# The half tile of features in the first products of the gated layer and of the experts, multiplied with 128 rows

## The chip, the cores and the metric

The kernel runs on one core of a Trainium2 chip. The core has five engines that run side by side, each with its own queue: TensorE (PE in the rows; its weight loads are listed apart as PEld), VectorE (DVE), ScalarE (ACT), GpSimd (POOL) and SyncE (SP). The metric is the device time of one launch in microseconds (us); lower is better. Times shown are medians of several runs; the profile is of one execution.

## The reference

Three layers follow each other on 4 batches of 768 tokens with 320 features.

```python
# 1. per head (8 heads of 40): a recurrence over the tokens
y[:, :, t] = einsum('bhd,bhde->bhe', rt, state)
Sa = einsum('bhde,bhe->bhd', state, at)
state = state * wt - outer(Sa, bt) + outer(vt, kt)
# 2. gated layer
h = maximum(x @ w_in, 0); u, v = h[..., :512], h[..., 512:]
v_n = (v - mean(v)) / sqrt(var(v) + 1e-6)
v_s = einsum('ts,bsd->btd', w_spatial, v_n) + b_spatial
x = (u * v_s) @ w_out
# 3. experts: the logits (with a local gate) choose one of 8 for each token
h = maximum(x[b, s] @ w1[e], 0)          # 320 -> 1024
out[b, s] = p[e] * (h @ w2[e])           # 1024 -> 320
```

The change concerns the two products whose contraction runs over the 320 features: `x @ w_in` and `x @ w1[e]`.

## The kernel before

**How a product is made exact enough.** The kernel multiplies in a shortened float32 format (float32r in the code). To keep float32's accuracy each operand is split into a high part, which the format holds, and a low part, the rest: x = xh + xl, W = WH + WL. A product is then the sum of three matmuls into one accumulator, WH xh + WL xh + WH xl; the term WL xl is left out.

**The 320 features** are two full tiles of 128 rows and half a tile of 64. The half tile is packed: the weights' tile 2 holds WH in its rows 0 to 63 and WL of the same features in rows 64 to 127, and the tokens' tile 2 holds the same 64 features twice. One matmul of 128 rows over (tile 2 of W, xh[2]) therefore gives WH xh + WL xh at once. What is missing is WH xl, and it is a second matmul over the rows 0 to 63 alone. So every group of first products has eight matmuls: three for each of the full tiles, one of 128 rows and, as the last, one of 64 rows.

**Where these groups stand.**
- Gated layer, `Gmlp.terms` (lines 796 to 804). `vprod` makes the v half, 128 tokens by 512 columns, six times per batch. `upart` makes the u half, 128 features of h by 384 tokens, eight times per batch. The matmuls' line in the profile is 795, that of the helper `mm`.
- Experts, `Moe.experts` (lines 1164 to 1294). A slot is 256 tokens of one expert (full) or 128 tokens (half); 17 slots always run, 12 full and 5 half, in the order F F, five times F F H, then further half slots that run only if they are needed. A full slot has eight groups of eight matmuls, one for each 128 rows of h, with the weights stationary and the 256 tokens moving (line 1245); then two products back to 320 columns, 24 matmuls each (`e_py`). A half slot has two groups of eight with the tokens stationary and 512 columns of weights moving (line 1264), four transposes for each, and one product back. The matmuls' line is 1200, that of the helper `products`.

**Tiles.** In the profile the gated layer's tokens go by reused buffers: xh are A32x, A32y, X32x and xl are X32y and two parts of XT1x, the second of which is xl[2]. The experts' tokens are xh and xl, the weights eWH and eWL, made from raw. The accumulators are pv, pu (gated layer, two buffers each), e_ph (four buffers) and e_py (two).

**What the other engines do beside it.** In the gated layer `splits` (line 735) makes xh on ScalarE and xl on VectorE (line 737); for the half tile xl is computed in rows 0 to 63 only, and rows 64 to 127 keep the unsplit features. v is normalized on VectorE (`vnorm`) and split again (`vsplit`: g_vh on ScalarE, g_vl on VectorE or GpSimd, line 837); the gated product `gated(i)` reads all six row blocks of g_vh and g_vl in order. In the experts `turn` transposes the gathered tokens of the next slot and splits them, with all 128 rows of xl[2]. A group of e_ph leaves through ScalarE (hh, line 1246) and VectorE (hl, line 1247). The weights of the slot after next are fetched by an indirect transfer (line 1173) and split in five pieces, each by a cast on ScalarE (line 1161) and a subtraction on VectorE (lines 1162 and 1163), put between the groups of the slot ahead.

**Order.** The attention's order is made by a list scheduler; the gated layer and the experts run in the order in which the code is written (`manual_schedule`), each engine taking its own instructions in turn.

Of the kernel before, what the change touches and what calls it, by code (L numbers as in the profile page):

```python
# [8 lines left out]
F32 = mybir.dt.float32  # L9
# [5 lines left out]
ALU = mybir.AluOpType  # L15
# [8 lines left out]
WW,AA,KB=0,264,520   # columns of the e-major record  # L24
EW=1032

def layout(r,k,v,w,a,b):
    """host: layout only"""
    f=np.float32
    def ch(x):  # (B,H,S,D)->(B,NC,pair,h,C,D)  # L30
        return x.reshape(B,NP,2,NC_,C,D).transpose(0,3,1,2,4,5)
    rc,kc,vc,wc,ac,bc=map(ch,(r,k,v,w,a,b))
    dm=lambda x: x.transpose(0,1,3,5,2,4)  # B,NC,h,D,pair,C
    e=np.zeros((B,NC_,RE,EW),f)
    # w: a zero, and per pair 64 values and a zero
    for h in range(2):
        rows=slice(64*h,64*h+40)
        we,ae,be,ke=(dm(x)[:,:,h] for x in (wc,ac,bc,kc))
        wz=np.zeros((B,NC_,40,NP,65),f); wz[...,:64]=we
        e[:,:,rows,WW+1:WW+261]=wz.reshape(B,NC_,40,260)  # L40
        e[:,:,rows,AA:AA+256]=ae.reshape(B,NC_,40,256)
        s0,s1=(be,ke) if h==0 else (ke,be)
        kb=np.stack([s0,s1],axis=4)  # B,NC,40,pair,slot,C
        e[:,:,rows,KB:KB+512]=kb.reshape(B,NC_,40,512)
    pw=np.ones((NP,65),f); pw[:,64]=0
    e[:,:,40:64,WW+1:WW+261]=pw.reshape(-1)
    # d-major: columns per pair V^T | R^T
# [6 lines left out]
    # t-major v of head 2p+1, with 16 rows of zeros after it, and of head 2p, with 16 before it  # L54
# [6 lines left out]
def attention(ctx,tc,ed,dd,vd,yT,order,K=KEYS,wp=None,prep=None,ident=None,guard=None):  # L61
    """ed,dd,vd as layout() gives; yT dram [320, B*S]"""
# [15 lines left out]
    ut=cp.tile([128,104],F32,name="ut")         # -1, in the first 64 columns only where s < t  # L78
# [37 lines left out]
    def heat(bank):  # L116
        # keeps the array's clock up while there is nothing to do
        if bank not in hcur: hcur[bank]=ps.tile([128,256],F32,name=bank)
        nc.tensor.matmul(out=hcur[bank],lhsT=hz[:,0:128],rhs=hz,start=True,stop=True)
    def tied(bank,n):  # L120
        # the same, but not before operation n has run
# [9 lines left out]
    nc.scalar.copy(hs,hz[:,0:2])       # has the engine's table loaded  # L131
# [7 lines left out]
    # ---- what does not depend on the state, chunk q of all heads of a batch  # L139
# [30 lines left out]
    def stM(q):  # L170
        # Q^T only; of A' the inversion reads nothing but what lies over its diagonal
# [14 lines left out]
    def stA(q):  # L186
        # once A' has left for the inversion, A-hat takes its place under (over) Q^T
        for sl,r in enumerate(halves): nc.scalar.copy(LQ[q][r,sl],AB[q%NAB][r,:,sl,:])
    # ---- inversion of the triangular matrices of n8 chunks
    def t32(ss):  # L190
# [7 lines left out]
        def load():  # L198
            # unit = (f, h, g, p); the 32x32 blocks on the diagonal
# [4 lines left out]
        def loadn():  # L204
            # and the block above
# [17 lines left out]
        def xtr():  # L223
            nc.scalar.copy(A32[ss][0:HU],X32[ss][0:HU].rearrange("p s t -> p t s"))   # A32 has done its work
# [17 lines left out]
    # ---- the chain of the chunks  # L242
# [91 lines left out]
    # ---- order: every engine takes, when it is free, the most urgent of what is ready by the estimates below  # L334
# [12 lines left out]
    if guard is not None:  # L347
        # in the room that the second inversion will take
# [67 lines left out]
    # list scheduling  # L416
# [11 lines left out]
    cols=dict(stQ=1672,stT=677,vr=324,s=643,z=1332,c1=78,c2=165,w=1644,t=845,y=1700)   # columns that the clock's monitor counts  # L428
# [12 lines left out]
    bank={b:-1. for b in ("pvr","pw","pc","pq","pk")}     # free since  # L441
# [48 lines left out]
    if K.get("xh"):  # L490
        # more of them where the chip waits longer than the estimates say
# [22 lines left out]
# attention() divides by the products of up to 64 decays: these must stay far from under- and overflow.  # L514
# A sum of exp(32 w) and one of exp(-32 w) over GN values bound each of them to 0.51 .. 1.29; values between 0.75 and 1.05 always pass.
# [3 lines left out]
def guard(nc,cp,wd):  # L519
    """(name, engine, time, after, time of transfer, function): whether any decay is out of the range, as an integer in flag"""  # L520
# [26 lines left out]
def general(ctx,tc,raw,yT,ident):  # L547
    """attention() for any decays: step by step, the state of 10 rows of a head on a partition"""
# [41 lines left out]
XW=392     # row of the token table: x2 | its last 64 columns again | 8 probabilities  # L590
# rows of x^T: tile 0 = heads 0,2,4 and 8 rows of head 6, tile 1 = heads 1,3,5 and 8 rows of head 7, tile 2 = the rest of 6 and 7
FEAT=np.concatenate([np.arange(40*h,40*h+n)+o for h,n,o in ((0,40,0),(2,40,0),(4,40,0),(6,8,0),(1,40,0),(3,40,0),(5,40,0),(7,8,0),(6,32,8),(7,32,8))])

def glayout(w_in,w_sp,b_sp,w_out,w_gate,w_local):
    f=np.float32
    # float64 goes as its bits
    wi=np.ascontiguousarray(w_in).view(np.int64)[FEAT]
    win=np.stack([wi[0:128],wi[128:256],np.concatenate([wi[256:320],wi[256:320]])],axis=1)  # 128,3,1024
# [5 lines left out]
class Gmlp:  # L604
# [4 lines left out]
    def narrow(self,src,raw,m,e,l):  # L609
        """src: dram, [128, n] bits of float64; its value as a sum of two float32, in m and l: (engine, name, function) by function"""  # L610
# [15 lines left out]
    def early(self,tmp):  # L626
        """the preparation that fits beside the end of the attention: (name, engine, time, after, time of transfer, function)"""
# [4 lines left out]
        def slot(tag): # what frees the next slot of the tag, and the operation that took the one before it  # L632
# [5 lines left out]
        def wi(k,h):  # L638
            """512 columns of a row tile of w_in"""
# [32 lines left out]
        def ws(c,n):  # L672
            """384 columns of a row tile of w_spatial"""
# [18 lines left out]
        # x of the first batch, where the inversions were  # L692
# [20 lines left out]
    def lload(self):  # L713
        """the last of w_spatial, where u will be"""
# [6 lines left out]
    def loads(self,b,eng=None):  # L721
        """x^T of a batch from y: (function, number of transfers)"""
# [12 lines left out]
    def splits(self,k):  # L735
        nc=self.nc; n=128 if k<2 else 64
        def lo(): nc.vector.tensor_tensor(out=self.xl[k][0:n],in0=self.xl[k][0:n].bitcast(F32),in1=self.xh[k][0:n].bitcast(F32),op=ALU.subtract)
# [5 lines left out]
    def weights(self,c1,gp):  # L743
        """what is left of the preparation; c1: context of what only the products before w_out need, gp: pool of the rest"""
# [5 lines left out]
        # the bias, on every partition  # L750
# [3 lines left out]
    def wout(self,ident,room):  # L754
        """w_out, with its product with the gate's weights beside it: (function before a product, function with it) four times"""
# [40 lines left out]
    def terms(self,tok,ff,tok_first):  # L796
# [6 lines left out]
        r+=[(xh[2],WH[2]),(xl[2][0:64],WH[2][0:64])]  # L803
        return r if tok_first else [(w,x) for x,w in r]
    def vprod(self,j):
        """the rows of 128 tokens before their normalization"""
# [17 lines left out]
    def vnorm(self,j):  # L824
# [4 lines left out]
        # 1/sqrt(var+eps), with a Newton step  # L829
# [13 lines left out]
    def biased(self,i):  # L843
        """what the products of gated(i) are added to"""
# [3 lines left out]
    def gated(self,i,gg,between=None):  # L848
        """between: what the array does next"""
# [13 lines left out]
    def out_(self,px,j,c,mid=None):  # L863
        """mid: what the array does in between"""
# [4 lines left out]
    def logits(self,LG,h,ident,lt):  # L869
        """LG [128,6,10]: the logits, and the local gate's, of half of the tokens"""  # L870
# [10 lines left out]
    def outp(self,j,xr,LG=None,mid=None):  # L881
        """xr [128,6,XW]: rows of the token table"""
# [8 lines left out]
SL=256            # tokens of a full slot  # L891
VE=3072//SL       # slots an expert can have
NF=12             # full slots
NH,NHA=8,5        # slots of half the tokens: at most, and those that always run
# [4 lines left out]
def mlayout(w1,w2):  # L899
    """(8*128, WC): per expert and partition, three tiles of rows of w1 (the last 64 rows twice) and eight of w2"""  # L900
# [4 lines left out]
class Moe:  # L905
# [10 lines left out]
    def fill(self):  # L916
# [21 lines left out]
        self.tok=cp.tile([128,24],F32,name="tok")      # 1 + the token's number  # L938
# [3 lines left out]
    def fill2(self):  # L942
        nc=self.nc; cp=self.tp
        # of the slots: bounds of the number in the list; number among the half slots and which half of a group (0 for the full ones)
# [19 lines left out]
    def route(self,b,LG,xr):  # L964
        """the stages of the routing of a batch: [what the vector engine begins with, then in turn products and what follows them]"""
# [8 lines left out]
        def begin(h):  # L974
# [8 lines left out]
            # the first of the largest logits  # L983
# [4 lines left out]
            # hold: 1/(1+exp(-z)) < 0.5 fails; in float32 that is 1+exp(-z) <= 2, and exp(-z) = 1-z where it matters  # L988
# [4 lines left out]
            # (8+fr)*(1-hold)  # L993
# [9 lines left out]
        def rows(n):  # L1003
            # half of the tokens, as two rows
# [17 lines left out]
        def places():  # L1022
            # place among the expert's tokens
# [28 lines left out]
    def first(self):  # L1052
        """the tokens of the first slot"""
# [9 lines left out]
    def heat(self,n,pu=None):  # L1063
        """products that nobody reads keep the array's clock up while it waits"""
        if pu is None: pu=self.ps.tile([128,384],F32,name="pu")
        for _ in range(n): self.nc.tensor.matmul(out=pu,lhsT=self.idb,rhs=self.i256.bitcast(BF16)[:,0:384],start=True,stop=True)
    def slots(self):
        """Which tokens and which expert a slot has. A list holds every expert's groups of 256 tokens (where the last may lack up to 127),
        then the rests of up to 128. The full slots take the list from its beginning; the half slots go on: two for a group, one for a rest."""
# [7 lines left out]
        # the first slot is the first expert's even if it has no tokens  # L1077
# [7 lines left out]
        # what the number in the list lacks to the number of the place  # L1085
# [15 lines left out]
    def slots2(self):  # L1101
# [4 lines left out]
        # the expert  # L1106
# [6 lines left out]
        # rows of the expert's weights; none where the buffer has them already  # L1113
# [6 lines left out]
        # the place  # L1120
# [13 lines left out]
    def numbers(self,ps):  # L1134
# [4 lines left out]
        # where the tokens are read from and written to; 4095 where there is none  # L1139
# [10 lines left out]
    def prefetch(self):  # L1150
        """the weights of the first slot"""
# [12 lines left out]
    def experts(self,ctx,out):  # L1164
# [36 lines left out]
        def run(lo,hi):  # L1201
            todo=[]
            def prepare(s):
                """the pieces of a slot's weights, to be split beside the slot before"""
# [24 lines left out]
            for s in range(lo,hi):  # L1229
# [7 lines left out]
                if n==2:  # L1237
                    for j in range(8):
# [6 lines left out]
                        products(ph,t+[(WH[:,c],xh[:,2]),(WH[0:64,c],xl[0:64,2])])  # L1245
# [6 lines left out]
                else:  # L1252
                    # the tokens stay in the array, the weights pass
# [3 lines left out]
                    for q in range(2):  # L1257
# [6 lines left out]
                        products(ph,t+[(xh[:,2,tk],WH[:,c]),(xl[0:64,2,tk],WH[0:64,c])])  # L1264
# [217 lines left out]
```

## Time and profile before

| | us |
|---|---|
| median of 3 runs | 1062.14 |
| lowest and highest run | 1059.57, 1075.4 |
| span of the profiled execution | 1064.1 |
| TensorE busy in it | 996.2 |
| VectorE busy | 752.6 |
| ScalarE busy | 585.2 |
| GpSimd busy | 444.6 |

The span goes from the first to the last instruction of one profiled execution; the page gives no other time for it. The busy time of TensorE counts overlapping matmuls once, and a matmul's end is modelled, so a busy TensorE can still be one that advances slowly: the distance between the starts of successive matmuls says how fast it goes. "PEclk" is the granted clock of TensorE as a share of full speed. An arrow in brackets names what ended an engine's idle time.

### The profile page before, as it was taken

What the parts mean: (1) busy time and instruction counts of PE and PEld (TensorE: products, weight loads), DVE (VectorE), ACT (ScalarE), POOL (GpSimd) and SP (SyncE); (2) the same over time, 40 slices, a digit from 0 to 9 for tenths busy, and PEclk for the clock granted to TensorE, in tenths of its full rate; (3) what the DMA queues carried; (4) which work ended last, traced back from release to release, by engine and by line L of the source; (5) the groups of instructions that cost most, each with busy time, mean ns of one, the idle gap of its engine ahead of it and who ended that gap; (6) DMA issues with size and microseconds to landing.
All of it is one profiled execution on the core that took longest, in us unless ns stands there. A gap on an engine that the chain in (4) does not pass through costs nothing. (4 is left out here: it accounts for less than half of the span.)

```text
span 1064.1 us, 25293 instructions
## 1 busy us (share of the span) xinstructions
PE 996.2 (94%) x9524; PEld 843.2 (79%) x9524; DVE 752.6 (71%) x2076; ACT 585.2 (55%) x1309; POOL 444.6 (42%) x624
## 2 busy tenths in 40 slices
PE   7898988888988999999999999999999999999995
PEld 6677777677877778876888888888878889888884
DVE  8989869998795999665765535654556666766672
ACT  7556656666766777773444324333435556655561
POOL 7886755756494621550431060220453232233211
PEclk8778978997977999999999999999999999999998
DMA  8756684765857664535200302101275643632530
GB/s 206 188 128 173 132 178 104 165 153 144 158 129 154 150 134 93 137 83 147 70 1 1 91 1 45 47 1 46 109 257 206 242 158 126 248 128 97 230 126 15
DMA packets 179055, 133.05 MB, mean 125 GB/s; under 512 B 132989, under 2 KB 165631, under 8 KB 177264
## 3 DMA queue, kind: packets, MB, share of 16 engines
q1 hardware_dynamic: 173376, 84.13, 33.2%
q0 software_dynamic: 5552, 47.25, 12.0%
q8 instruction: 77, 1.26, 0.5%
q14 instruction: 50, 0.41, 0.1%
HBM read 113.54 MB, written 27.26 MB: 132 GB/s over the span
## 5 line engine op out<-in xcount | busy, mean ns | idle before, releaser
L219 DVE TENSOR_TENSOR pr<-A,X 128x30 f32<-128x30 f32 (+40 forms) x427 | 114.8, 307 | 4.1 <-POOL AB L161 3.3
L222 DVE TENSOR_TENSOR X<-X,pr 128x30 f32<-128x30 f32 (+40 forms) x427 | 112.3, 302 | 0.2
L1163 DVE TENSOR_TENSOR eWL<-raw,eWH 128x1024 fp32r<-128x1024 f32 (+1 forms) x64 | 86.4, 1358 | 33.7 <-ACT eWH L1161 33.4
L1161 ACT CAST eWH<-raw 128x1024 fp32r<-128x1024 f32 (+1 forms) x85 | 94.0, 1134 | 0.0
L1290 POOL DMA_INDIRECT out_dram<-yo,sid x29 | 29.6, 1020 | 147.5 <-ACT yo L1289 108.1
L1200 PE MATMUL e_ph<-xl,eWH 128*128 128x256 f32 (+1 forms) x288 | 90.5, 314 | 0.2 <-DVE xl L1191 0.2
L1200 PE MATMUL e_ph<-xh,eWH 128*128 128x256 f32 x288 | 89.9, 312 | 0.0
L173 POOL TENSOR_SCALAR_AFFINE_SELECT lq<-lq 64x256 f32<-64x256 f32 x96 | 67.2, 700 | 50.8 <-DMA pu<-lq 29.6
L157 POOL TENSOR_TENSOR kb<-etile,Ft 104x256 f32<-104x256 f32 x88 | 71.3, 830 | 41.1 <-DVE D L149 24.6
L1200 PE MATMUL e_py<-eWH,hh 128*128 128x320 f32 x232 | 73.0, 315 | 0.0
L322 PE MATMUL py<-X,kt 128*64 128x104 f32 x384 | 56.1, 286 | 17.9 <-DVE X L317 17.9
L1200 PE MATMUL e_py<-eWH,hl 128*128 128x320 f32 x232 | 72.3, 312 | 0.2 <-DVE hl L1273 0.2
L1200 PE MATMUL e_py<-eWL,hh 128*128 128x320 f32 x232 | 71.6, 309 | 0.0
L1246 ACT ACTIVATE hh<-e_ph 128x256 fp32r<-128x256 f32 x96 | 37.0, 385 | 62.6 <-PE e_ph L1200 61.3
L1247 DVE SCALAR_TENSOR_TENSOR hl<-e_ph,hh 128x256 fp32r<-128x256 f32 x96 | 39.6, 422 | 42.8 <-ACT hh L1246 42.8
L857 PE MATMUL pv<-sh,g_vh 128*128 128x384 f32 x192 | 67.1, 350 | 0.0
L161 POOL TENSOR_TENSOR AB<-etile,GP 64x256 f32<-64x256 f32 x82 | 62.9, 767 | 7.2 <-issue 2.2
L857 PE MATMUL pv<-sl,g_vh 128*128 128x384 f32 x192 | 64.8, 337 | 0.0
L857 PE MATMUL pv<-sh,g_vl 128*128 128x384 f32 x192 | 64.7, 337 | 0.0
L1200 PEld LDWEIGHTS e_ph<-xl,eWH 128*128 128x128 f32 (+1 forms) x288 | 53.9, 187 | 12.7 <-DVE xl L1191 0.4
L165 PE MATMUL pq<-AB,kb 104*128 104x128 f32 x384 | 63.7, 318 | 0.1
L1200 PEld LDWEIGHTS e_ph<-xh,eWH 128*128 128x128 f32 x288 | 54.0, 187 | 11.6 <-DVE eWH L1162 0.3
(350 smaller groups left out, 2984.5 us busy)
## 6 DMA issues: line engine op xcount, KB each, us to landing
etile<-in_ed_dram SPq DMA_DIRECT2D x48, 419.2 KB
DT<-in_dd_dram SPq DMA_DIRECT2D x96, 80.0 KB
pu<-lq SPq DMA_DIRECT2D x96, 80.0 KB
yT<-yt SPq DMA_DIRECT2D x48, 104.0 KB
X<-in_vd_dram SPq DMA_DIRECT2D x96, 50.0 KB
XT<-in_w_dram SPq DMA_DIRECT2D x10, 384.0 KB
xs<-xr SPq DMA_DIRECT2D x3, 1176.0 KB
praw<-in_win_dram SPq DMA_DIRECT2D x6, 512.0 KB
```

The lines of the kernel that those rows point to most:

```text
L157: eng.tensor_tensor(out=kb[:,:,sl,:],in0=kbr[:,:,sl,:],in1=FT[q][:,::-1,63::-1],op=ALU.mult)
L161: eng.tensor_tensor(out=AB[q%NAB][r,:,sl,:],in0=ar[r],in1=GP[q%NBIG][r,:,0:64],op=ALU.mult)
L165: nc.tensor.matmul(out=PQ[q][:,p,:],lhsT=kbt[q][:,p].rearrange("p s t -> p (s t)"),rhs=AB[q%NAB][0:RE,p].rearrange("p s t -> p (s t)"),sta ...
L173: nc.gpsimd.affine_select(out=LQ[q][r,h],in_=LQ[q][r,h],pattern=[[0,NP],[1,64]],**sel)
L219: nc.vector.tensor_tensor(out=pv,in0=a[0:U,0:t,t:t+1].to_broadcast([U,t,c1-c0]),in1=x[0:U,t:t+1,c0:c1].to_broadcast([U,t,c1-c0]),op=ALU.mult)
L222: nc.vector.tensor_tensor(out=x[0:U,0:t,c0:c1],in0=x[0:U,0:t,c0:c1],in1=pv,op=ALU.subtract)
L322: nc.tensor.matmul(out=py[0:64,p,:],lhsT=KT[q][:,p,0:64],rhs=x[:,p,0,:],start=False,**acc)
L857: for j,(l,r) in enumerate(t): nc.tensor.matmul(out=pv,lhsT=l,rhs=r,start=False,stop=j==len(t)-1,skip_group_check=True)
L1161: nc.scalar.copy(WH[:,c0:c1],raw[:,c0:c1])
L1163: else: V.tensor_tensor(out=WL[:,lc(c0):lc(c1)],in0=raw[:,c0:c1],in1=WH[:,c0:c1].bitcast(F32),op=ALU.subtract)
L1200: for i,(l,r) in enumerate(t): nc.tensor.matmul(out=out,lhsT=l,rhs=r,start=i==0,stop=i==len(t)-1)
L1247: V.scalar_tensor_tensor(out=hl[:,j],in0=ph,scalar=0.0,in1=hh[:,j].bitcast(F32),op0=ALU.max,op1=ALU.subtract)
```

## The change

The matmul of the half tile's low part takes 128 rows of both operands and not 64. In its rows 64 to 127 it adds WL xl for the half tile's features, the term that is left out elsewhere. In the gated layer the subtraction that makes xl[2] runs over 128 rows too, so that these rows hold low parts; in the experts they did already. The number and the order of the instructions on every engine stay the same; four subtractions of line 737 (and a fifth that runs only in the fallback for extreme decays) and 162 matmuls with their weight loads change their number of rows. The rest of the diff removes comments.

```diff
@@ Gmlp.splits, line 735
-        nc=self.nc; n=128 if k<2 else 64
-        def lo(): nc.vector.tensor_tensor(out=self.xl[k][0:n],in0=self.xl[k][0:n].bitcast(F32),in1=self.xh[k][0:n].bitcast(F32),op=ALU.subtract)
+        nc=self.nc
+        def lo(): nc.vector.tensor_tensor(out=self.xl[k],in0=self.xl[k].bitcast(F32),in1=self.xh[k].bitcast(F32),op=ALU.subtract)
@@ Gmlp.terms, line 803
-        r+=[(xh[2],WH[2]),(xl[2][0:64],WH[2][0:64])]
+        r+=[(xh[2],WH[2]),(xl[2],WH[2])]
@@ Moe.experts, full slot, line 1245
-                        products(ph,t+[(WH[:,c],xh[:,2]),(WH[0:64,c],xl[0:64,2])])
+                        products(ph,t+[(WH[:,c],xh[:,2]),(WH[:,c],xl[:,2])])
@@ Moe.experts, half slot, line 1264
-                        products(ph,t+[(xh[:,2,tk],WH[:,c]),(xl[0:64,2,tk],WH[0:64,c])])
+                        products(ph,t+[(xh[:,2,tk],WH[:,c]),(xl[:,2,tk],WH[:,c])])
```

## Rows read from the trace of the kernel before

**Rows 1.** The page of the profiled execution: its span.

```profile
span 1064.1 us, 25293 instructions
```

**Rows 2.** Busy time by stretch: us, then each engine (x instructions), granted clock, DMA, GB/s.

```profile
492.50:1051.50 559.00, 552.91 (x3223) 471.53 (x3224) 336.48 (x758) 265.21 (x504) 154.61 (x211) 1.00 0.32 111
510.60:522.50 11.90, 11.90 (x56) 9.08 (x56) 11.24 (x28) 7.10 (x17) 5.81 (x14) 1.00 0.02 4
```

**Rows 3.** TensorE's timeline, experts, full slot: start us, duration us, engine, line, output and operands.

```profile
802.43 0.31 PE L1200 MATMUL e_py<-eWH,hl 128*128 128x320 f32 x1
802.58 0.28 PE L1200 MATMUL e_ph<-xh,eWH 128*128 128x256 f32 x1
...
803.29 0.28 PE L1200 MATMUL e_ph<-xh,eWH 128*128 128x256 f32 x1
803.50 0.38 PE L1200 MATMUL e_ph<-xl,eWH 64*128 64x256 f32 x1
803.81 0.39 PE L1200 MATMUL e_ph<-xh,eWH 128*128 128x256 f32 x1
804.03 0.28 PE L1200 MATMUL e_ph<-xl,eWH 128*128 128x256 f32 x1
```

**Rows 4.** Groups by line and shape, the matmuls of 64 rows: busy us, mean ns.

```profile
L1200 PE MATMUL e_ph<-xl,eWH 64*128 64x256 f32 x96 | 36.6, 382 | 0.0
...
L795 PE MATMUL pu<-XT1x,wh 64*128 64x384 f32 x32 | 14.1, 441 | 0.0
...
L795 PE MATMUL pv<-wh,XT1x 64*128 64x512 f32 x24 | 11.9, 496 | 0.0
...
L1200 PE MATMUL e_ph<-eWH,xl 64*128 64x512 f32 x10 | 5.0, 496 | 0.0
```

**Rows 5.** TensorE's timeline, last u product of the first batch and the gated product behind it.

```profile
520.62 0.34 PE L795 MATMUL pu<-X32y,wh 128*128 128x384 f32 x1
...
521.31 0.34 PE L795 MATMUL pu<-X32x,wh 128*128 128x384 f32 x1
521.58 0.44 PE L795 MATMUL pu<-XT1x,wh 64*128 64x384 f32 x1
521.95 0.44 PE L857 MATMUL pv<-sh,g_vh 128*128 128x384 f32 x1
522.23 0.33 PE L857 MATMUL pv<-sl,g_vh 128*128 128x384 f32 x1
```

**Rows 6.** TensorE's timeline, experts, a half slot.

```profile
858.43 0.40 PE L1200 MATMUL e_ph<-eWH,xh 128*128 128x512 f32 x1
858.75 0.50 PE L1200 MATMUL e_ph<-eWH,xl 64*128 64x512 f32 x1
...
859.51 0.39 PE L1200 MATMUL e_ph<-eWH,xl 128*128 128x512 f32 x1
...
860.67 0.40 PE L1200 MATMUL e_ph<-eWH,xh 128*128 128x512 f32 x1
```

**Rows 7.** Line 737 by tile: durations min/median/max ns, first and last start, shapes.

```profile
L737 DVE TENSOR_TENSOR XT1x<-XT1x,A32y x4: 950/954/958, 490.5 to 673.2; 128x768 fp32r<-128x768 f32 x4
L737 DVE TENSOR_TENSOR XT1x<-XT1x,X32x x4: 940/941/944, 491.8 to 677.3; 64x768 fp32r<-64x768 f32 x4
```

**Rows 8.** GpSimd's timeline, first batch: the last low part for gated(0).

```profile
523.13 1.29 POOL L837 TENSOR_TENSOR g_vl<-g_v,g_vh 128x512 fp32r<-128x512 f32 x1 [2.24 <-ACT g_vh L836]
```

**Rows 9.** The page's costliest groups: busy us, mean ns, idle before and its releaser.

```profile
L1163 DVE TENSOR_TENSOR eWL<-raw,eWH 128x1024 fp32r<-128x1024 f32 (+1 forms) x64 | 86.4, 1358 | 33.7 <-ACT eWH L1161 33.4
...
L1247 DVE SCALAR_TENSOR_TENSOR hl<-e_ph,hh 128x256 fp32r<-128x256 f32 x96 | 39.6, 422 | 42.8 <-ACT hh L1246 42.8
```

**Rows 10.** Transfers into the tiles raw from 760 us on.

```profile
DMA to landing us min/median/max: 2.1/10.7/11.5
```

**Rows 11.** GpSimd's timeline: the issue of one slot's weights.

```profile
921.95 1.01 POOL L1173 DMA_INDIRECT raw<-in_wt_dram,wid  x1 [3.73 <-DVE eWL L1163]
```

**Rows 12.** ScalarE's timeline: the first read of these weights.

```profile
937.18 1.04 ACT L1161 CAST eWH<-raw 128x1024 fp32r<-128x1024 f32 x1
```


## The prediction, made before the result was known

> **What bounds the kernel now.** I read the busy time by stretch first. From 492.5 us, where the first product of the gated layer starts, to 1051.5 us, where the last product of the experts ends, TensorE is busy 552.91 of 559.00 us, at a granted clock of 1.00 (the 2.4 GHz level) throughout; VectorE is busy 336 us of it and ScalarE 265 us [rows 2]. The span is 1064.1 us [rows 1]. So in this stretch what TensorE does not have to do leaves the span, as long as the engines with 60% and 47% keep up.
>
> A busy TensorE need not be a productive one, so the second view is its timeline, read by starts and not by durations (matmuls overlap). Within a group of e_ph the starts of 256-column matmuls are (803.29 - 802.58)/6 = 0.118 us apart [rows 3]. Then comes the matmul that the change edits, xl against eWH with 64 rows: it starts 0.21 us after its predecessor, the next one 0.31 us after it, and the one behind that 0.22 us later [rows 3]. Three steps that would take 0.354 us at the normal pace take 0.74: **0.386 us are lost around one matmul of 64 rows**. A group's end is not the cause: from the last e_py to the first e_ph, another group, another tile, both with 128 rows, it is 0.15 us, no more than the 320 columns need [rows 3]. Nor is it a wait for xl: two of the six steps between 802.58 and 803.29 begin 128-row matmuls of xl.
>
> The same hole is there at other widths and with operands exchanged. 384 columns, in the u products: normal pace (521.31 - 520.62)/4 = 0.173; from 521.31 to 522.23 it is 0.92 against 0.519, a loss of 0.40 [rows 5]. 512 columns, in a half slot, where the tokens are stationary: normal (860.67 - 859.51)/5 = 0.232; from 858.43 to 859.51 it is 1.08 against 0.696, a loss of 0.384 [rows 6]. The loss does not grow with the columns: it is a fixed price for going from 128 rows to 64 and back. I take 0.39 us.
>
> **The change part by part.** No instruction is added, removed or moved. The second operand pair of one product per group gets 128 rows, and the split of xl[2] in the gated layer does 128 rows, so that the other 64 hold low parts and not unsplit features (in the experts they are split already).
>
> *The matmuls.* There are 96 + 32 + 24 + 10 = 162 of them [rows 4]. With 128 rows each has the form of its neighbours, which run without the hole. What they still cost is the neighbours' pace, already in the 0.354. So 162 x 0.39 = 63.2 us: 106 in the experts (41.3) and 56 in the gated layer (21.8). Bounds: 0.384 x 162 = 62.2 and 0.40 x 162 = 64.8; nothing would be gained if the hole had another cause (a rival below).
>
> The Trainium skill, in "TensorEngine Tiling (Array Packing)", section Key Properties, says that changing the tiling mode drains the engine. That fits the hole on both sides of the 64-row matmul, but gives no figure; the sum goes by the rows.
>
> *The split of xl[2].* On 64 rows it takes 941 ns, the same operation on 128 rows for xl[1] 954 ns [rows 7]: 0.013 us, four times, on VectorE. I take nothing. At the worst, if the added rows cost as much again, 0.9 us before the first product, and three times beside products.
>
> *What is late next, gated layer.* In the first batch the u products are followed at 521.95 by gated(0) [rows 5], which reads the six normalized row blocks in order; the last block's low part is made on GpSimd from 523.13 for 1.29 us, to 524.42 [rows 8]. gated(0) needs it at its eighteenth matmul, 521.95 + 17 x 0.173 = 524.9: there is half a microsecond of cover now. Its makers work through VectorE, which from 510.60 to 522.50 is busy 11.24 of 11.90 us [rows 2]: this chain doesn't shrink with TensorE. I estimate that it ends 1.7 us earlier, at 522.7: its first statistics follow the first v product and start 0.39 earlier, the 0.66 us in which VectorE is idle in this stretch may close, and I allow as much again for gaps ahead of it. TensorE would be there 14 x 0.39 = 5.5 us earlier and get only 524.9 - 522.7 = 2.2. So **3.3 us of the 5.5 are not gained**; 0 if the chain moves with TensorE, 5 if it doesn't move at all. In later batches the normalization is spread over the output products before and has more time.
>
> *What is late next, experts.* Per group of e_ph VectorE does hl, 0.422 us, and behind every other group a piece of the next slot's weights, 1.358 us [rows 9]. Two groups with a piece: 2.20 us. TensorE takes 2 x (8 x 0.118 + 0.386) = 2.66 us for two groups now and will take 1.89. VectorE then falls back 0.31 us per pair, and there are two pairs with a piece in a full slot, three in the four full slots that follow a half one: 0.62 or 0.93 us per slot. e_ph has four buffers, so TensorE can be three groups, 2.8 us, ahead, and in the e_py part, which isn't shortened, VectorE makes it up. I put 1 us for the whole stage, with bounds of 0 and the full lag, 8 x 0.62 + 4 x 0.93 = 8.7 us.
>
> *The weights' transfers.* A slot's weights take 10.7 us to land in the median and 11.5 at most [rows 10]. One of the tightest is issued at 921.95 [rows 11] and first read at 937.18 [rows 12], 15.2 us later, so 3.7 us are spare against the longest. Of this stretch some six holes of 0.39 go, 2.3 us, so even the longest still lands 1.4 us before it is needed. I take nothing; a transfer that took 2 us more than the longest would cost 0.6 us per slot, about 8 us in 13.
>
> **The sum.** 63.2 - 3.3 - 1.0 = 58.9 us off the profiled span: 1064.1 - 58.9 = 1005.2 us. That execution stands 2.0 us above the median of the runs, 1062.14, so the forecast is 1062.1 - 58.9 = **1003 us**.
>
> **The rivals.**
> *Nothing is gained.* If the hole came from what these matmuls read or from where they stand, 128 rows would keep it: 1062 us. For it: the 64-row matmul is always the last of its group. Against it: three widths, both operand orders and two successors (a group of the same kind, a gated product) show the same 0.39, and the group end with 128 rows on both sides shows none. The Trainium skill, "TensorE: Matmul & The Clock Gate", section LDWEIGHTS (loading the stationary operand), says that the number of rows doesn't matter for the load's time, only the columns; by that rule alone the change does nothing. The profile agrees as far as durations go, but the starts decide here. Chance 0.04.
> *Lag in the experts.* VectorE's lag isn't absorbed, or transfers come late: 8.7 us are given back instead of 1.0, 1062.1 - 58.9 + 7.7 = 1011 us. For it: VectorE will be slower than TensorE in the e_ph part. Against: four buffers, and the e_py part of every slot in which it catches up. Chance 0.12.
> *Slower.* The wait at gated(0) opens holes in TensorE's work near 520 us, and the granted clock, 1.00 now [rows 2], falls to the 1.2 GHz level. Each microsecond of work done there instead of at 2.4 GHz costs 0.5 of elapsed time per elapsed microsecond, so 59 us are eaten only if 118 us run at the low level; beyond 160 us of it the kernel would be slower by 2%, 1083 us. A short fall of 10 us costs 5 us: 1008. For it: one stretch with gaps that isn't there now. Against: the products behind it are dense. Chance 0.04 for a short fall, 0.01 for a long one.
>
> **How the numbers follow.** The forecast (no lag, 996 to 1008) has 0.79, lag 0.12, short fall 0.04, nothing gained 0.04, slower 0.01. The range for 8 in 10 starts at the full 64.8 us from the lowest run shown, 1059.6 - 64.8 = 995, and goes to the lag's full bound, 1011, with 2 us for the distance between a single execution and the median, 1013. A measurement of this kernel tells about 2% from no change (its three runs span 1.5%). Faster by more than 2% (below 1041): 0.79 + 0.12 + 0.04 = 0.95; same 0.04; slower 0.01.
>
> **What would show it.** In the changed kernel's timeline the eighth matmul of e_ph starts 0.118 us after the seventh and the next group 0.118 us after that; the e_ph part of a full slot falls from 8 x 1.33 us by 8 x 0.386 to 7.55. The u products take 8 x 1.39 us and not 1.79. TensorE waits some 3 us at the first gated product and nearly nowhere else, and its clock stays at 1.00. I am wrong if the starts still show 0.2 and 0.3 us around the edited matmul, if TensorE waits at every slot's e_ph for VectorE or for a transfer, or if the clock falls behind 520 us.

## The result, and the profile after

The changed kernel took 1012.19 us in the median of four runs (1009.6 to 1019.1), the kernel before, measured beside it, 1062.06: a ratio of 0.9554, 95% interval 0.9507 to 0.9602, **faster**. By this ratio the 1062.1 of the forecast's reference become 1014.8 us. The forecast was 1003, its range 995 to 1013, so the result lies 1.8 us above the range. Two later measurements of the same two kernels gave 0.9394 (0.9343 to 0.9445) and 0.9408 (0.9354 to 0.9462), 997.8 and 999.2 us of the same 1062.1. The ratios leave out runs far above the fastest of their kernel, while the medians given here and below are over all runs. Why three measurements of one pair differ by more than their intervals is the main matter of what follows.

The holes are gone. This is TensorE's timeline of the changed kernel in a full slot (columns as in [rows 3]):

```profile
786.38 0.31 PE L1200 MATMUL e_py<-eWH,hl 128*128 128x320 f32 x1
786.52 0.28 PE L1200 MATMUL e_ph<-xh,eWH 128*128 128x256 f32 x1
...
787.23 0.28 PE L1200 MATMUL e_ph<-xh,eWH 128*128 128x256 f32 x1
787.35 0.28 PE L1200 MATMUL e_ph<-xl,eWH 128*128 128x256 f32 x1
787.47 0.28 PE L1200 MATMUL e_ph<-xh,eWH 128*128 128x256 f32 x1
787.58 0.28 PE L1200 MATMUL e_ph<-xl,eWH 128*128 128x256 f32 x1
```

The edited matmul is the one at 787.35. It starts 0.12 us after its predecessor, its successor 0.12 us after it; in [rows 3] these were 0.21 and 0.31. The half slot, to be held against [rows 6]:

```profile
833.83 0.39 PE L1200 MATMUL e_ph<-eWH,xh 128*128 128x512 f32 x1
834.05 0.39 PE L1200 MATMUL e_ph<-eWH,xl 128*128 128x512 f32 x1
834.28 0.39 PE L1200 MATMUL e_ph<-eWH,xh 128*128 128x512 f32 x1
```

The steps around the edited matmul, at 834.05, are 0.22 and 0.23 us. Next come the span and the busy time by stretch as in [rows 2]: the gated layer from its first matmul to the first e_ph, the experts from there to the start of the last e_py, and 3.4 us of the first batch:

```profile
span 1010.7 us, 25299 instructions
```

The six instructions more than in [rows 1] are semaphore instructions, three in TensorE's and three in VectorE's queue.

```profile
495.89:770.26 274.37, 266.37 (x1555) 244.01 (x1555) 165.18 (x505) 113.03 (x258) 79.92 (x140) 0.99 0.19 56
770.26:998.30 228.04, 226.62 (x1672) 220.02 (x1671) 167.03 (x254) 150.05 (x246) 93.72 (x72) 1.00 0.55 205
527.50:530.90 3.40, 3.40 (x12) 3.40 (x12) 2.70 (x8) 1.36 (x4) 0.00 (x0) 0.50 0.05 10
```

The two stages that the change touches take 274.37 + 228.01 = 502.4 us; in the trace of before the same two took 290.57 + 268.62 = 559.2 (that is the stretch of [rows 2], to the start of the last e_py). They gained **56.8 us; the forecast was 58.9.** The tail behind them is 12.4 us in both. The attention ahead of them, whose code is the same, ended at 495.89 us and not at 492.50.

This is the place where the forecast put a wait, the gated product of the first batch:

```profile
520.04 0.34 PE L795 MATMUL pu<-XT1x,wh 128*128 128x384 f32 x1
521.59 0.45 PE L857 MATMUL pv<-sh,g_vh 128*128 128x384 f32 x1 [1.21 <-ACT pv L847]
521.87 0.34 PE L857 MATMUL pv<-sl,g_vh 128*128 128x384 f32 x1
...
522.92 0.34 PE L857 MATMUL pv<-sl,g_vh 128*128 128x384 f32 x1
523.35 0.44 PE L857 MATMUL pv<-sh,g_vl 128*128 128x384 f32 x1
...
524.33 0.34 PE L857 MATMUL pv<-sl,g_vh 128*128 128x384 f32 x1
525.04 0.45 PE L857 MATMUL pv<-sh,g_vl 128*128 128x384 f32 x1 [0.38 <-DVE g_vl L837]
...
526.44 0.44 PE L857 MATMUL pv<-sh,g_vl 128*128 128x384 f32 x1 [0.61 <-POOL g_vl L837]
526.73 0.82 PE L788 MATMUL px<-g_rawg,XT0x 128*128 128x10 f32 x6
527.48 0.69 PE L857 MATMUL pv<-sh,g_vh 128*128 128x384 f32 x1
527.97 0.52 PE L857 MATMUL pv<-sl,g_vh 128*128 128x384 f32 x1
528.28 0.52 PE L857 MATMUL pv<-sh,g_vl 128*128 128x384 f32 x1
...
531.06 0.34 PE L857 MATMUL pv<-sh,g_vl 128*128 128x384 f32 x1
531.23 0.34 PE L857 MATMUL pv<-sh,g_vh 128*128 128x384 f32 x1
```

gated(0) starts 1.55 us after the last u product (0.37 in [rows 5]), because ScalarE's copy into pv comes late, and stops three times more, each time ahead of a product with a low part of v: at 523.35 (0.43 us behind its predecessor and not 0.17), at 525.04 and at 526.44. From 527.97 the starts are 0.31 to 0.33 us apart and not 0.17: the granted clock is 0.50, the 1.2 GHz level, until 530.9. The low parts that TensorE waits for stand in VectorE's and GpSimd's timelines:

```profile
521.50 1.79 DVE L837 TENSOR_TENSOR g_vl<-g_v,g_vh 128x512 fp32r<-128x512 f32 x1
...
524.30 0.68 DVE L837 TENSOR_TENSOR g_vl<-g_v,g_vh 128x512 fp32r<-128x512 f32 x1
```

```profile
521.23 1.51 POOL L837 TENSOR_TENSOR g_vl<-g_v,g_vh 128x512 fp32r<-128x512 f32 x1 [1.33 <-ACT g_vh L836]
525.12 1.27 POOL L837 TENSOR_TENSOR g_vl<-g_v,g_vh 128x512 fp32r<-128x512 f32 x1 [2.38 <-ACT g_vh L836]
```

The last of them, at 525.12 on GpSimd, answers to [rows 8]. TensorE could have taken it one step behind its seventeenth matmul of this product, some 0.8 us before 526.44.

### The profile page after: what moved, and what is told of

Same layout as the page of the kernel before. It is cut to its first block, busy times and chain, and to the rows that moved or that the text cites. A ratio compares the mean times of both kernels' runs of the same rounds, so it can differ in the third digit from the quotient of the medians.

```text
span 1010.7 us, 25299 instructions
## 1 busy us (share of the span) xinstructions
PE 939.9 (93%) x9524; PEld 835.6 (83%) x9524; DVE 739.8 (73%) x2076; ACT 582.3 (58%) x1309; POOL 465.3 (46%) x624
## 5 line engine op out<-in xcount | busy, mean ns | idle before, releaser
L219 DVE TENSOR_TENSOR pr<-A,X 128x30 f32<-128x30 f32 (+40 forms) x427 | 112.1, 301 | 3.4 <-DMA A<-pu 2.7
L222 DVE TENSOR_TENSOR X<-X,pr 128x30 f32<-128x30 f32 (+40 forms) x427 | 108.1, 292 | 0.2
L157 POOL TENSOR_TENSOR kb<-etile,Ft 104x256 f32<-104x256 f32 x88 | 72.7, 847 | 50.8 <-DVE D L149 21.8
L1290 POOL DMA_INDIRECT out_dram<-yo,sid x29 | 41.6, 1434 | 107.5 <-ACT yo L1289 37.5
L173 POOL TENSOR_SCALAR_AFFINE_SELECT lq<-lq 64x256 f32<-64x256 f32 x96 | 63.1, 657 | 51.6 <-DMA pu<-lq 41.8
L1200 PE MATMUL e_ph<-xh,eWH 128*128 128x256 f32 x288 | 76.9, 281 | 0.0
L1200 PE MATMUL e_ph<-xl,eWH 128*128 128x256 f32 x288 | 76.4, 278 | 0.2 <-DVE xl L1191 0.2
L165 PEld LDWEIGHTS pq<-AB,kb 104*128 104x128 f32 x384 | 56.7, 227 | 6.8 <-POOL AB L161 2.5
L322 PE MATMUL py<-X,kt 128*64 128x104 f32 x384 | 52.5, 276 | 9.9 <-DVE X L317 9.8
L314 PE MATMUL pw<-Wt,XT 64*64 64x104 f32 x768 | 48.8, 269 | 8.4 <-ACT Wt L308 4.5
L282 POOL TENSOR_SCALAR_AFFINE_SELECT X<-X 64x256 f32<-64x256 f32 x48 | 25.5, 530 | 64.6 <-ACT X L278 45.0
```

Of the source, the lines that this page charges most:

```text
L157: eng.tensor_tensor(out=kb[:,:,sl,:],in0=kbr[:,:,sl,:],in1=FT[q][:,::-1,63::-1],op=ALU.mult)
L165: nc.tensor.matmul(out=PQ[q][:,p,:],lhsT=kbt[q][:,p].rearrange("p s t -> p (s t)"),rhs=AB[q%NAB][0:RE,p].rearrange("p s t -> p (s t)"),sta ...
L173: nc.gpsimd.affine_select(out=LQ[q][r,h],in_=LQ[q][r,h],pattern=[[0,NP],[1,64]],**sel)
L219: nc.vector.tensor_tensor(out=pv,in0=a[0:U,0:t,t:t+1].to_broadcast([U,t,c1-c0]),in1=x[0:U,t:t+1,c0:c1].to_broadcast([U,t,c1-c0]),op=ALU.mult)
L222: nc.vector.tensor_tensor(out=x[0:U,0:t,c0:c1],in0=x[0:U,0:t,c0:c1],in1=pv,op=ALU.subtract)
L314: nc.tensor.matmul(out=pw[r0:r0+64,p,:],lhsT=xt_(q)[r0:r0+64,p,:],rhs=w[r0:r0+64,p,:],start=True,stop=True)
```

## The experiments

All times below that are called stages come from profiles: the gated layer from its first matmul to the first e_ph, the experts to the start of the last e_py. "Low" is the time, summed over the attention, in which the trace gives TensorE a granted clock of 0.50, the 1.2 GHz level; it gives no value but 0.50 and 1.00. All figures are us.

| kernel | attention ends | low | gated layer | experts |
|---|---|---|---|---|
| before | 492.5 | 105.8 | 290.57 | 268.62 |
| changed | 495.9 | 112.6 | 274.37 | 228.01 |
| e1 experts only | 488.7 | 99.0 | 290.61 | 227.47 |
| e2 gated layer only | 492.4 | 95.6 | 272.76 | 268.64 |
| e3 changed, again | 509.0 | 150.2 | 274.39 | 227.99 |
| e4 pairs of 64 rows | 485.5 | 99.0 | 290.53 | 250.40 |
| e5 96 rows | 485.2 | 81.9 | 290.61 | 232.16 |
| e6 low parts on VectorE | 492.3 | 105.8 | 270.92 | 227.77 |
| e7 filled waits | 490.7 | 112.6 | 272.85 | 228.98 |
| e8 both | 502.5 | 139.9 | 272.43 | 228.64 |
| e9 e6, again | 496.1 | 116.1 | 271.17 | 228.30 |
| e10 changed, a third time | 491.6 | 92.2 | 272.90 | 227.23 |

**One half of the change at a time.** e1 is the kernel before with the two lines of the experts, e2 with those of the gated layer.

```diff
+ e1: products(ph,t+[(WH[:,c],xh[:,2]),(WH[:,c],xl[:,2])])
+ e1: products(ph,t+[(xh[:,2,tk],WH[:,c]),(xl[:,2,tk],WH[:,c])])
+ e2: r+=[(xh[2],WH[2]),(xl[2],WH[2])]
- e2: nc=self.nc; n=128 if k<2 else 64
+ e2: nc=self.nc
+ e2: def lo(): nc.vector.tensor_tensor(out=self.xl[k],in0=self.xl[k].bitcast(F32),in1=self.xh[k].bitcast(F32),op=ALU.subtract)
```

> Only the experts' products (lines 1245 and 1264) get 128 rows; the gated layer keeps its 64. Theory (a fixed price for each excursion from 128 rows to 64 and back): 96 + 10 holes of 0.39 us go, 41.3 us, less about 1 us in which a slot's weights come late; the e_ph part of a full slot 7.3 to 7.5 us instead of 10.5, of a half slot 3.7 instead of 4.4; the gated layer as before. Time about 1062 - 40 = 1022 us (ratio 0.962), if the attention's length differs between runs by chance alone. Rival (the change makes the attention longer by the 7 us that the medians suggest): 1029 us.

> Only the gated layer's products (line 803 and the split of line 735) get 128 rows. Theory: 56 holes of 0.39 us, 21.8 us, less 3.7 us of waits in the first batch (gated(0) and the u products before it) and 1.6 us if the granted clock falls behind them: 16.5 to 18 us, 1044 to 1046 us (ratio 0.983 to 0.985). Rival (the change makes the attention longer): about 1052 us.

e1 took 1020.96 us, ratio 0.9505 (0.9449 to 0.956); its experts gained 41.2 us and its gated layer nothing. e2 took 1055.83 us, ratio 0.9826 (0.976 to 0.9893), which alone leaves open whether it is 2% faster; its gated layer gained 17.8 us and its experts nothing. The kernel before, measured beside them, took 1072.78 us in the median and not 1062, so that e1 met its expected time and missed its ratio by 0.012, while e2 met its ratio and missed its time by 10 us, nearer to the rival's 1052. The totals can't decide here, the stages can: each stage's gain is that of its own lines, and they add up to 17.8 + 41.2 = 59.0 us. That is 2.2 us more than the changed kernel gained in the same stages in its first profile, and as much as it gained in e10 below (59.1). e2 had the waits at gated(0) without a fall of the clock.

**The changed kernel, again.**

> The changed kernel once more, for the length of the attention. From the first product of the gated layer to the last product of the experts both theories expect 498.5 us as in its first profile (555.3 before). If the attention's length is chance: median about 1062 - 56.8 = 1005 us (ratio 0.947). If the change makes the attention longer: 1012 us again (0.953).

Its time was 1007.76 us in the median of six runs (999.63 to 1025.42), ratio 0.9394. The profiled execution was the longest of the six, a span of 1023.8 us, and yet the two stages took 274.39 and 227.99 us, within 0.02 of the first time. All 13 us of the difference lie in the attention. The attention stands below in four profiles, in order e3, the changed kernel, its third profile e10, and e5 (the figure behind the five counts of instructions is the granted clock):

```profile
0.00:509.04 509.04, 459.59 (x6300) 384.41 (x6300) 408.61 (x1319) 318.88 (x804) 282.73 (x412) 0.85 0.61 139
```

```profile
0.00:495.89 495.89, 446.64 (x6300) 371.52 (x6300) 407.56 (x1319) 318.70 (x804) 290.71 (x412) 0.89 0.63 143
```

```profile
0.00:491.63 491.63, 438.20 (x6299) 364.29 (x6300) 412.07 (x1319) 317.96 (x804) 278.28 (x412) 0.91 0.63 144
```

```profile
0.00:485.18 485.18, 433.27 (x6300) 362.23 (x6300) 411.10 (x1319) 318.54 (x804) 283.36 (x412) 0.92 0.63 146
```

The same 6300 matmuls take 485 to 509 us, the longer the lower the mean granted clock. TensorE's idle time in these four, the length less the busy time, is 49.5, 49.3, 53.4 and 51.9 us: it is the busy time that grows. Over the twelve profiles of the table the attention's end grows by 0.32 us for each microsecond at the low level (correlation 0.93; 0.25 and 0.72 without the two longest, e3 and e8). The times that were not profiled go the same way: of the 33 runs of the kernel before that were measured beside these experiments, the longest, 1081.2 us, had a mean granted clock of 0.929 over the whole program and the shortest, 1058.6 us, one of 0.959 (correlation -0.94). None of the edits touches the attention's products, and nothing here shows that the change makes it longer.

**What exactly costs the hole?** e4 keeps all 64-row matmuls, but puts them first in every second group of a full slot, so that two of them stand side by side: as many of them, half as many changes of rows. e5 gives those of the full slots 96 rows.

```diff
- products(ph,t+[(WH[:,c],xh[:,2]),(WH[0:64,c],xl[0:64,2])])
+ e4, even j: products(ph,t+[(WH[:,c],xh[:,2]),(WH[0:64,c],xl[0:64,2])])
+ e4, odd j:  products(ph,[(WH[0:64,c],xl[0:64,2])]+t+[(WH[:,c],xh[:,2])])
+ e5:         products(ph,t+[(WH[:,c],xh[:,2]),(WH[0:96,c],xl[0:96,2])])
```

> The kernel before with another order in the full slots alone: in every second group of e_ph the matmul of 64 rows comes first instead of last, so that two of them stand side by side across the group's boundary; as many matmuls of 64 rows, half as many excursions. Theory (price per excursion): four holes of about 0.39 us per slot instead of eight, e_ph part 9.0 instead of 10.5 us, 48 x 0.39 = 18.7 us less in all, about 1043. Rival (price per matmul of 64 rows, whatever stands beside it): unchanged, about 1062.

> The kernel before with 96 rows instead of 64 in the low-part matmul of the full slots alone. Theory A (only the step from the whole array to half of it costs): 96 rows run as 128 do, no hole, the stretch from the experts' first product to their last falls from 268.6 by 96 x 0.39 = 37 to about 232 us. Theory B (any change of the number of rows costs): the holes stay, 268.6 us.

e4 took 1040.42 us and e5 1022.25, one run each; the stages and the starts decide. Here is TensorE's timeline of e4 (x2 is the pair), then of e5:

```profile
784.92 0.28 PE L1200 MATMUL e_ph<-xh,eWL 128*128 128x256 f32 x1
785.04 0.28 PE L1200 MATMUL e_ph<-xh,eWH 128*128 128x256 f32 x1
785.24 0.49 PE L1200 MATMUL e_ph<-xl,eWH 64*128 64x256 f32 x2
785.66 0.39 PE L1200 MATMUL e_ph<-xh,eWH 128*128 128x256 f32 x1
785.89 0.28 PE L1200 MATMUL e_ph<-xl,eWH 128*128 128x256 f32 x1
```

```profile
783.30 0.28 PE L1200 MATMUL e_ph<-xh,eWH 128*128 128x256 f32 x1
783.41 0.28 PE L1200 MATMUL e_ph<-xl,eWH 96*128 96x256 f32 x1
783.53 0.28 PE L1200 MATMUL e_ph<-xh,eWH 128*128 128x256 f32 x1
```

In e4 one pair costs, from 785.04 to 785.89, 0.85 us for four steps of 0.117: a hole of 0.38, as large as that of a single one. The experts gained 18.2 us with 48 fewer excursions, 0.38 each. So the price is that of going to 64 rows and back, not of the matmul, and it does not hang on the matmul's being the last of its group. In e5 the edited matmul has no hole on either side and the experts take 232.2 us, 36.5 less: 96 x 0.38, with the half slots still at 64 rows. Fewer than 128 rows is therefore not the cause; the step to 64 is. The Trainium skill, "TensorEngine Tiling (Array Packing)", lists 128, 64 and 32 rows under Available Configurations and says under Key Properties that changing the mode drains the engine; these two runs agree, and put 0.38 us on one excursion. The drain itself is seen in no view; what they show is the price and that 96 rows don't pay it.

**The wait in the first batch.** e6 makes all low parts of the first batch on VectorE and has ScalarE fill pv ahead of its casts of v. e7 leaves these as changed and puts products that nobody reads into the waits ahead of the first, ninth, fifteenth and eighteenth matmul of gated(0). e8 does both, with three fewer of these products.

```diff
+ e6, e8: if i == 1:
+ e6, e8:     G.biased(0)
- G.vsplit(i - 2, G.nc.gpsimd if i % 2 else None)
+ e6, e8: G.vsplit(i - 2)
- if i == 5:
-     G.biased(0)
...
+ e7: hn = {0: 6, 8: 3, 14: 4, 17: 5}
+ e8: hn = {0: 3, 8: 3, 14: 4, 17: 5}
+ e7, e8: fill = lambda j: M.heat(hn.get(j, 0), hp)
...
  for j,(l,r) in enumerate(t):
+ e7, e8: if fill: fill(j)
```

> The changed kernel; in the first batch all six low parts of v are made on VectorE (three of them were on GpSimd) and the copy of the bias for gated(0) stands ahead of the casts of v on ScalarE. Theory (in the first batch the chain over VectorE and GpSimd, not TensorE, sets when gated(0) ends): VectorE works off 6 x 0.6 us of low parts without being slowed by GpSimd's, the last low part comes about 2 us earlier, and the stretch from the gated layer's first product to the experts' falls from 274.4 to about 272.3 us, or 270.7 if the granted clock stays at 1.00. Rival (TensorE itself is the limit there): 274.4 or, with the clock at 1.00, 272.8 us.

> The changed kernel; where TensorE waits around gated(0) of the first batch it makes 18 products that nobody reads, between those of gated(0). Theory (the granted clock fell at 527.5 us because TensorE had gaps before it): the clock stays at 1.00 until the experts end, gated(1) and gated(2) take 6.4 us together and not 7.95, and the stretch from the gated layer's first product to the experts' falls from 274.4 to about 272.8 us. Rival (the fall has nothing to do with the gaps): it comes again, 274.4 us.

> The changed kernel with the low parts on VectorE, the earlier copy of the bias and 15 such products in gated(0). Theory: both gains together, 270.7 us from the gated layer's first product to the experts' (274.4 in the changed kernel), 228.0 us for the experts; in time 3 to 4 us less than the changed kernel, which the attention's scatter hides in single runs: about 1004 us against 1008, ratio to the kernel before about 0.936.

e6 (1004.97 us, one run): gated(0) begins 0.18 us behind the last u product and ends 29.05 us after the stage's start; in the changed kernel it was 30.84, before it 32.70. One long wait is left:

```profile
516.43 0.34 PE L795 MATMUL pu<-XT1x,wh 128*128 128x384 f32 x1
516.61 0.34 PE L857 MATMUL pv<-sh,g_vh 128*128 128x384 f32 x1
...
519.87 0.44 PE L857 MATMUL pv<-sh,g_vl 128*128 128x384 f32 x1 [0.90 <-DVE g_vl L837]
```

The stage takes 270.92 us, 2.0 less than in e10, which had the same clock of 1.00. So about half of the wait came from the division of the low parts among the engines and the late copy, which e6 changes together, not from the length of the chain as such. e7 (1006.76 us, one run) kept the clock at 1.00 and took 272.85 us, as expected; but e2 and e10 kept it with the waits unfilled, so e7 doesn't show that the filling did it. e8 (1015.99 us, 0.9496, 0.9427 to 0.9566) missed its expectation by 1.7 us in the stage and by 12 in time: with the low parts earlier, the fifteen added products themselves hold gated(0) up, which ends 30.45 us after the start against 29.05 in e6. Its higher time is, as far as its profile shows, the attention's (502.5 us).

**Both versions side by side,** on one chip and against the same eleven runs of the kernel before:

> The same kernel as in the look with the low parts of the first batch all on VectorE, now timed in five rounds. Theory (the gain lies in the stages behind the attention, and the attention's own length scatters with its time at the low granted clock): the gated layer 270.9 and the experts 227.8 us in its profile, as before, so 60.5 us under the kernel before by the stages ((290.57 + 268.62) - (270.92 + 227.77)), a ratio near 0.943 against pooled times of the kernel before of some 1067, with an interval about 0.006 to each side. Rival (the short profile of the first look was an accident of a good attention, and the low parts on VectorE do nothing): stages as in the changed kernel, 274.4 and 228.0, and a ratio near 0.947.

> The changed kernel once more, on the same chip and against the same runs of the kernel before as the version with the low parts on VectorE. Theory: its gated layer and experts take 274.4 and 228.0 us again, whatever its attention takes, and over enough executions its ratio is near 1 - 56.8/1067 = 0.947. Rival (the gain itself changes from execution to execution): the two stretches differ from these by over 1 us while its total moves.

e9 took 1009.49 us (999.65 to 1024.77), ratio 0.939 (0.9323 to 0.9457), stages 271.17 + 228.30. e10 took 1004.96 us (1001.99 to 1017.67), ratio 0.9408 (0.9354 to 0.9462), stages 272.90 + 227.23. The gated layer of e6 was repeated within 0.25 us, but in the time its gain can't be seen: the two intervals lie over each other. By the stages e6 and e9 are the shortest versions (498.7 and 499.5 us; e10 500.1, the changed kernel 502.4). That the gain in the stages doesn't change holds to 2.3 us and no better, as e10's rival had it: its gated layer is 1.47 us shorter than in the changed kernel's first profile, where the clock fell behind gated(0), and its experts are 0.78 us shorter. Of the three profiles of the changed kernel, one shows that fall; e3 has one of the same length, 3.4 us, 2.3 us after the stage's start, so that its gated layer agrees with the first profile's to 0.02 us by accident.

## Why the prediction was right and wrong

**What held.** *The mechanism and its price.* The forecast took away 162 holes of 0.39 us. They are gone at 256 and 512 columns, as shown above; at 384 columns the u products of a later batch take 11.10 us and not 14.19, 0.386 for each of eight. e4 and e5 confirm that it is a price per excursion. *The experts:* 41.3 - 1.0 = 40.3 us were forecast; it was 40.6, 40.6 and 41.4 in the three profiles of the changed kernel, 41.2 in e1. A full slot's e_ph part takes 7.26 to 7.74 us where 7.55 was forecast (the first one, among other small products, 8.57). VectorE's lag, the term of 1.0 with its bound of 8.7, was practically nothing, as the 41.4 of e10 show; what was lost in the first profile was a transfer, the term put at zero. These are the waits of TensorE behind the attention, those of the gated product and of the experts (the first was there before, at 1.2 us):

```profile
PE e_px L1187 <- DMA xg<-xs,gid: 1.4, 1, 1.4
...
PE pv L857 <- ACT pv L847: 1.2, 1, 1.2
...
PE e_py L1200 <- DVE hl L1247: 0.6, 1, 0.6
PE pv L857 <- POOL g_vl L837: 0.6, 1, 0.6
...
PE pv L857 <- DVE g_vl L837: 0.4, 1, 0.4
```

The wait of 0.6 for hl follows from a transfer of weights. Below are its issue on GpSimd (at 797.98), ScalarE's first read of it, and TensorE's wait:

```profile
797.98 1.45 POOL L1173 DMA_INDIRECT raw<-in_wt_dram,wid  x1 [0.30 <-issue]
...
803.28 1.02 POOL L1173 DMA_INDIRECT raw<-in_wt_dram,wid  x1 [2.51 <-DVE eWL L1163]
```

```profile
808.89 1.05 ACT L1161 CAST eWH<-raw 128x1024 fp32r<-128x1024 f32 x1 [2.96 <-DMA raw<-in_wt_dram,wid]
```

```profile
813.39 0.41 PE L1200 MATMUL e_py<-eWH,hl 128*128 128x320 f32 x1 [0.65 <-DVE hl L1247]
```

The cast waits 2.96 us for weights issued 10.9 us before; the evictions of e_ph queue behind it, and this slot's e_py part takes 8.05 us and not 7.13. That is once in 17 slots, 0.9 us; e9 has one in another slot, e3 one of 0.6, e10 none. The 15.2 us of [rows 11, 12], less 2.3, were not the tightest case once the slots came faster: this cast was due 8.0 us after the issue (808.89 - 2.96 - 797.98), and the longest landing in this profile took 12.6 us, not 11.5.

*The wait in the first batch:* 3.3 us were forecast. gated(0) ends 30.84 us after the stage's start and not 32.70, so of 14 x 0.39 = 5.5 us 1.9 were gained and 3.6 were not. The place and the size were right, and so nearly was the chain: its last low part ended 1.4 us earlier in the stage (525.12 + 1.27 - 495.89 = 30.5, before 523.13 + 1.29 - 492.50 = 31.9) where 1.7 were estimated. What the forecast did not see is that TensorE waits along the whole product and not at its eighteenth matmul alone: 1.4 us ahead of the first, for ScalarE's copy into pv, and 2.0 inside (526.73 - 521.59 = 5.14 us for 18 matmuls that need 3.1 at 0.173). The copy was no part of the chain that the forecast followed.

**What came out otherwise.** *The gated layer:* 21.8 - 3.3 = 18.5 us were forecast; 16.2 were measured in the first profile, 17.7 in e10 and 17.8 in e2. The fall of the clock, the rival with a chance of 0.04, did come in that execution: 3.4 us at half speed, 1.5 us lost. It can be seen in one of four profiles with the unfilled waits (the changed kernel three times, and e2), so 0.04 looks too little; its price, 5 us for 10 at the low level, was put nearly right. Together the stages gained 56.8, 56.8 and 59.1 us in the three profiles, of 58.9. That the 59.1 of e10 meet the forecast so closely is in part luck: the experts gave 1.1 us more than forecast, the gated layer 0.8 less.

**The step that failed** is the last of the range: "2 us for the distance between a single execution and the median", and with it the sum's reference, a median of three runs. These three spanned 16 us, with a standard deviation of 8.5, and that was read only as a bound on what can be told from no change. The runs of this kernel scatter with a standard deviation of 6.5 us (37 runs), and in the profiles such a scatter lies in the attention, which takes 485 to 509 us by the clock that it is granted. In all, 37 runs of the kernel before have a median of 1067.1 us (1058.6 to 1081.2) and 16 of the changed one 1009.6 (999.6 to 1025.4). The difference, 57.5 us, is of the size of the stages' 56.8 to 59.1. Of the 9.0 us between 1012.2 and the 1003.2 forecast, 5.0 are by these medians the reference (1062.1 for 1067.1), 2.6 the four runs of the result (1012.2 for 1009.6) and 1.4 the gain. By the scatter such medians are good to some 2 us (an estimate), so this last figure is not told from nothing. By the first profiles alone: 1064.1 - 58.9 = 1005.2 was forecast for the span; 1010.7 came, 3.4 us of it in the attention and 2.1 in the gain. A time of a run, moreover, is its span and 1.5 us (1012.2 for the profiled 1010.7), so the profiled execution of before stood nearer to 3.5 than to 2.0 us above the median of the three. An upper end that allowed one standard deviation of the reference and of four new runs, some 5 us, would have been 1016.

What stays open is why an attention with the same instructions has 82 us at the low level in one execution and 150 in another, and whether the waits at gated(0) or something else decide whether the clock falls behind them. No run here tells these apart. The three measurements of the pair may also differ by the chip: the two later ones were made on two different chips, and that of the first is not on record.

## What to carry to other kernels

Read a busy engine by the starts of its instructions: where one shape breaks the pace on both sides, price the break by the excursion, not by the instruction, and make the operand the shape of its neighbours, with zeros or a useful term in the added rows. Forecast the stage and the reference apart: a stage far from the change can scatter by more than the change's smaller terms, so compare the touched stages between profiles, and take the range of the total from the spread of the runs, not from a median of three. A stage that loses its slack should have every transfer's time from issue to first read listed, not one that looks tight.

## What the runs showed of the hardware

- An excursion from 128 rows to 64 and back costs TensorE 0.38 to 0.40 us at 256, 384 and 512 columns, and at 256 columns as much for one matmul as for two in a row; at 256 columns an excursion to 96 rows costs nothing.
- VectorE's subtraction g_vl takes 0.68 us alone and 1.79 beside the same operation on GpSimd (1.51 there, 1.27 alone). The Trainium skill, "SBUF — State Buffer", section Who interferes with whom, says that a VectorE instruction with two inputs in SBUF contends with a GpSimd one that reads SBUF; the rows above agree. In the kernel before these two met for 0.14 us only, and its 21 on VectorE took at most 0.69; but beside GpSimd's g_vl (515.74 and 519.62) VectorE's small operation of line 830 took 1.24 and 1.23 us there, and 0.20 to 0.22 the other 22 times.
- The granted clock of a stage with gaps, the attention, was 0.85 to 0.92 over twelve executions of the same instructions, and its length followed, 509 to 485 us.
